# One core, block-sorted attention and a gated MLP: all units in a new order, with other PSUM tiles and copying engines, k loaded before v, and Sinkhorn's matrix kept by rows

## The chip, the core and the metric

The kernel runs on one core of one Trainium2 chip. The core has five engines with their own instruction streams: TensorE (PE in the profile; PEld is its loading of weights), VectorE (DVE), ScalarE (ACT), GpSimd (POOL) and SyncE (SP, which only issues DMAs here). DMAs are issued from SP, ACT and POOL. The metric is device time in microseconds (us) of the whole program, and lower is better. A profiled execution gives a span, the time from the first to the last instruction that the profile shows; the program's own time is a little longer.

## What is computed

The reference, cut to what matters, with 4 batches, 8 heads, 768 tokens, head size 64, 8 blocks of 96 tokens, and a hidden width of 1024:

```python
for _ in range(5):                       # P: one 8 x 8 matrix per batch and head
    P = np.exp(P - np.max(P, axis=-1, keepdims=True))
    P = P / (np.sum(P, axis=-1, keepdims=True) + 1e-09)
    P = P / (np.sum(P, axis=-2, keepdims=True) + 1e-09)
k_sorted = np.einsum('bhij,bhjcd->bhicd', P, k_b)      # blocks mixed by P
v_sorted = np.einsum('bhij,bhjcd->bhicd', P, v_b)
scores = scale * np.matmul(q_b, k_sb.transpose(0, 1, 2, 4, 3))   # inside a block
attn = softmax(scores)
x = np.matmul(attn, v_sb)                # heads side by side: 768 x 512 per batch
h = np.maximum(x @ w_in, 0.0)
u, v = h[..., :512], h[..., 512:]
v_n = (v - mean(v)) / np.sqrt(var(v) + 1e-06)
v_s = np.einsum('ts,bsd->btd', w_spatial, v_n) + b_spatial[None, :, None]
out = (u * v_s) @ w_out
```

## The kernel before, in words

The whole work is cut into some 360 small units, and their order is written out by hand in the string ORDER (lines 18 to 51). A unit is a name and its arguments. The kernel walks through the string and calls the function u_NAME for each (lines 789 to 801), so the string fixes the order of the instructions on every engine at once. Each engine works through its own instructions strictly in that order and waits by semaphores for what it needs.

Most units of PE take one of four PSUM tiles, ps0 to ps3 (line 105, two banks each, one buffer each), fill it with matmuls, and name the engine that copies it out: A is ScalarE, D is VectorE. So `KT:3:D:0:0` is: mix k of batch 0, heads 0 and 1, by P and turn it, in ps3, copied out by VectorE. The next unit on ps3 can't start before that copy has ended. The numbers and letters in the string are thus the choice of tile and engine.

The units that the change and the prediction speak of:

- L loads a tensor by POOL with a cast to bf16 (lines 165 to 188): q, k or v of one batch (768 KB in bf16), the u and v halves of w_in (wu, wv), two halves of w_spatial (wsa, wsb), w_out (wo). LH (349) loads half of q of batch 0 on ACT's queue in fp32, and QC (356) casts it. BI loads the bias; IV (223) sets the columns of ones beside v. Eight semaphores serve POOL's loads in turn, so a load waits on POOL for the landing of the eighth load before it.
- SK (234) is one round of Sinkhorn, on 32 partitions (batch and head) by 64 numbers: an exponential on ACT, and row sum, reciprocal, multiply, column sum, reciprocal, multiply on VectorE. S0 loads sort_net. TB, CO, ID, MA, MB, MC prepare tables, zeros, the identity and masks. DM (227) are matmuls on zeros that keep PE going until the data are there.
- PR (257) spreads P over the partitions, P0 (271) makes the mixing matrices of batch 0 on VectorE, PC (280) copies P out of PSUM, and PD (283) makes those of the other batches on POOL.
- QT and QQ (323, 329) turn q of one or two pairs of heads; QP and QX (362, 373) do this for batch 3 by a copy and a DMA transpose. KT and VT (395, 398) mix and turn k and v; VB (401) turns the mixed v back, for batch 0. For the other batches VM (411) mixes v without turning, and VC (425) moves it to its place (vb) by eight DMAs of 99 KB, on SP's queue.
- SC (439) are the scores of a pair of heads and half of the blocks (eight matmuls, then an exponential by ACT); AT (484) multiplies with v (eight matmuls, then reciprocal and multiply on VectorE, into x).
- XT and XX (516, 541) turn x on PE, XD (507) does it by a DMA transpose on SP.
- VP (552) is the v half of x @ w_in for one or two of six token tiles, UP (594) the u half; ST, LN, LA (570, 579, 585) normalize v; WT and WW (526, 532) turn w_spatial; SP (609) is the product with w_spatial, whose sum with the bias VectorE makes; GT (626) the gating on VectorE (D) or POOL (P); OP, OE, OS (634, 647, 653) the last product, its copy and its store.
- SH, GH, OH, OI, OJ (665 to 702) do the last of batch 3 in finer pieces. CK, CF, LF (713, 728, 734) test that Sinkhorn and softmax stayed in range and load the flag; IF is the branch on it, and general_path (743) is taken if they did not.

In the order before, the head is the Sinkhorn chain beside dummy matmuls; then comes the attention of batch 0 with the mixing of v of batch 1 in between; then the attention of each batch is interleaved with the MLP of the batch before it. The first VP stands in line 27.

## Times and profile before

| | |
|---|---|
| time, median of 3 runs | 155.43 us (155.09 to 156.04) |
| time of the profiled execution | 155.6 us |
| span of the profiled execution | 153.8 us |
| busy share of the span: PE, DVE, ACT, POOL | 95%, 75%, 56%, 26% |
| granted TensorE clock, mean | 0.996 |
| dummy matmuls (DM) | 33, 461 ns each |
| bytes read from HBM, written | 24.78 MB, 6.29 MB |
| DMA engines' busy share, first 18 slices of 40 | 0.9 after the first one |

The profile divides the span into 40 slices of 3.85 us and gives each engine's busy share in tenths. A row of the timeline has a start, a length, an engine, a line of the kernel, an operation with output and inputs, and how many; in brackets stands how long the engine sat idle before it and what ended that. Lines 115, 117, 121 and 123 are the helpers that copy for all units, so their rows are told apart by tile and shape. The chain that ended last is PE for 85% of the span and DMA for 7%, the DMA being the first load of k.

### The profile page before, as it was taken

What the parts mean: (1) busy time and instruction counts of PE and PEld (TensorE: products, weight loads), DVE (VectorE), ACT (ScalarE), POOL (GpSimd) and SP (SyncE); (2) the same over time, 40 slices, a digit from 0 to 9 for tenths busy, and PEclk for the clock granted to TensorE, in tenths of its full rate; (3) what the DMA queues carried; (4) which work ended last, traced back from release to release, by engine and by line L of the source; (5) the groups of instructions that cost most, each with busy time, mean ns of one, the idle gap of its engine ahead of it and who ended that gap; (6) DMA issues with size and microseconds to landing.
All of it is one profiled execution on the core that took longest, in us unless ns stands there. A gap on an engine that the chain in (4) does not pass through costs nothing.

```text
span 153.8 us, 4021 instructions
## 1 busy us (share of the span) xinstructions
PE 146.5 (95%) x1679; PEld 95.6 (62%) x1686; DVE 115.7 (75%) x259; ACT 85.4 (56%) x116; POOL 39.3 (26%) x45
## 2 busy tenths in 40 slices
PE   6997998999999999999999999999999999999991
PEld 2436866764667777456777654656876556774750
DVE  3789889958899976299974886797977639855742
ACT  4345998877879245997777057357650072260040
POOL 7952772292020007000000044000000406103630
PEclk9999999999999999999999999999999999999998
DMA  3999999999999999991069048708608300307746
GB/s 100 251 203 203 204 205 204 210 219 248 220 208 256 203 232 245 208 194 24 0 158 134 19 104 161 190 0 38 191 14 258 121 0 0 136 0 268 288 181 235
DMA packets 30693, 24.36 MB, mean 158 GB/s; under 512 B 10384, under 2 KB 27792, under 8 KB 30672
## 3 DMA queue, kind: packets, MB, share of 16 engines
q0 software_dynamic: 14432, 12.19, 49.1%
q1 hardware_dynamic: 15136, 10.44, 26.4%
q10 hardware_dynamic: 1104, 1.44, 2.8%
q8 instruction: 14, 0.23, 0.6%
q14 instruction: 7, 0.06, 0.1%
HBM read 24.78 MB, written 6.29 MB: 202 GB/s over the span
## 4 chain that ended last, share of the span: by engine, by line
PE 85%; DMA 7%; ACT 2%; DVE 2%; issue 1%; POOL 1%; POOLq 0%; ACTq 0%
PE ps L614 15%; PE ps L559 14%; PE ps L602 14%; PE ps L640 10%; DMA k_in<-in_k_dram 7%; PE ps L493 5%; PE ps L447 5%; PE ps L670 5%; PE ps L388 4%; PE ps L690 3%; PE ps L319 2%; PE ps L415 2%; PE ps L523 2%; ACT ex_all L452 2%; PE ps L536 1%
## 5 line engine op out<-in xcount | busy, mean ns | idle before, releaser
L631 POOL TENSOR_TENSOR gt<-z,u_sb 128x768 bf16<-128x768 f32 x7 | 11.4, 1642 | 76.7 <-DVE z L620 47.4
L452 ACT ACTIVATE ex_all<-ps 96x768 bf16<-96x768 f32 x32 | 24.7, 806 | 5.6 <-PE ps L447 5.3
L614 PE MATMUL ps<-wspT,v_sb 128*128 128x384 bf16 x144 | 25.1, 326 | 0.0
L602 PE MATMUL ps<-xT,w_in_sb 128*128 128x384 bf16 x128 | 22.8, 326 | 0.0
L501 DVE TENSOR_TENSOR x_sb<-ps,rec_all 96x512 bf16<-96x512 f32 x32 | 22.0, 687 | 1.1
L559 PE MATMUL ps<-w_in_sb,xT 128*128 128x512 bf16 x89 | 21.9, 380 | 0.4
L576 DVE BATCH_NORM_STATS2 stats<-v_sb 128x6 f32<-128x512 bf16 x24 | 16.3, 678 | 4.5 <-ACT v_sb L121 4.5
L115 ACT COPY o_sb<-ps 128x1024 f32<-128x1024 f32 (+1 forms) x12 | 10.9, 905 | 14.6 <-PE ps L690 9.1
L614 PEld LDWEIGHTS <-v_sb 128*128 128x128 bf16 x144 | 13.6, 98 | 8.5
L121 ACT ACTIVATE v_sb<-ps 128x1024 bf16<-128x1024 f32 (+1 forms) x11 | 10.3, 947 | 12.2 <-PE ps L559 12.2
L640 PE MATMUL ps<-w_out_sb,gt 128*128 128x256 bf16 x144 | 16.9, 273 | 0.0
L121 ACT ACTIVATE u_sb<-ps 128x768 bf16<-128x768 f32 x12 | 9.7, 811 | 12.7 <-PE ps L602 12.7
L620 DVE TENSOR_TENSOR z<-ps,b_bc 128x768 f32<-128x768 f32 x12 | 11.4, 954 | 6.9 <-PE ps L614 5.1
L602 PEld LDWEIGHTS <-w_in_sb 128*128 128x128 bf16 x128 | 11.8, 97 | 7.2
L640 PEld LDWEIGHTS <-gt 128*128 128x128 bf16 x144 | 13.8, 98 | 2.0
L559 PEld LDWEIGHTS <-xT 128*128 128x128 bf16 x96 | 8.7, 98 | 9.9
L493 PEld LDWEIGHTS <-ex_all 96*128 96x128 bf16 x256 | 10.7, 97 | 4.0 <-issue 0.5
L493 PE MATMUL ps<-vb,ex_all 96*128 96x65 bf16 x256 | 12.6, 193 | 0.5 <-ACT ex_all L452 0.5
L230 PE MATMUL ps<-warm 128*128 128x512 bf16 x33 | 9.7, 461 | 1.3 <-DVE warm L204 1.3
L447 PE MATMUL ps<-qT,kt_all 64*128 64x96 bf16 x256 | 9.7, 204 | 0.7 <-DVE x_sb L501 0.2
L115 ACT CAST kt_all<-ps 128x768 bf16<-128x768 f32 x11 | 8.7, 801 | 2.2 <-PE ps L388 2.2
L447 PEld LDWEIGHTS <-kt_all 64*128 64x128 bf16 x256 | 6.4, 94 | 5.3 <-issue 3.2
...
## 6 DMA issues: line engine op xcount, KB each, us to landing
...
v_in<-in_v_dram POOLq DMA_DIRECT2D x4, 768.0 KB, 21.0
k_in<-in_k_dram POOLq DMA_DIRECT2D x4, 768.0 KB, 23.6
vb<-vm SPq DMA_DIRECT2D x24, 99.0 KB, 5.7
q_in<-in_q_dram POOLq DMA_DIRECT2D x3, 768.0 KB, 28.9
...
w_in_sb<-in_moe_w_in_dram POOLq DMA_DIRECT2D x2, 512.0 KB, 24.7
q<-in_q_dram ACTq DMA_DIRECT2D x1, 768.0 KB, 4.6
```

The lines of the kernel that those rows point to most:

```text
L115: nc.scalar.copy(out=out, in_=in_)
L121: nc.scalar.activation(out=out, in_=in_, func=AF.Relu)
L447: nc.tensor.matmul(t[:, hh, 0:HW].rearrange("p (g x) -> p g x", g=G)[:, :, ii * TB:(ii + 1) * TB], lhsT=kT[rows, i * BLK:i * BLK + 128], r ...
L452: nc.scalar.activation(out=e_tile(b, hp, ih).rearrange("p h (x g) -> p h x g", g=G), in_=t[0:BLK, :, 0:HW].rearrange("p h (g x) -> p h x g ...
L493: nc.tensor.matmul(t[:, hh, ii * VW:ii * VW + D + 1], lhsT=e[:, c:c + 128], rhs=vb[b % 2][:, ih * NI + ii, 2 * hp + hh, 0:D + 1], start=Tr ...
L501: nc.vector.tensor_mul(out=x_sb[:, hp].rearrange("p i (h d) -> p h i d", h=2), in0=tv[:, :, :, 0:D], in1=_raw_ap(rec, 0, [rec.ap[0], [NI, ...
L559: nc.tensor.matmul(t[:, x, :], lhsT=st["xT", b][:, n // 3, kc, (n % 3) * 128:(n % 3 + 1) * 128], rhs=w_in_sb[:, kc, DH:DFF], start=(kc == ...
L576: nc.vector.bn_stats(out=stats, in_=st["v_sb", b, n])
L602: nc.tensor.matmul(t[:, x, 0:HW], lhsT=w_in_sb[:, kc, mc * 128:(mc + 1) * 128], rhs=st["xT", b][:, ih, kc, :], start=(kc == 0), stop=(kc = ...
L614: nc.tensor.matmul(t[:, x, 0:HW], lhsT=st["v_sb", b, n][:, mc * 128:(mc + 1) * 128], rhs=wspT[:, 3 * x:3 * x + 3, n, :], start=(n == 0), s ...
L620: nc.vector.tensor_add(out=z.rearrange("p (x c) -> p x c", x=2), in0=t[:, :, 0:HW], in1=b_bc.rearrange("p (x c) -> p x c", x=2),)
L640: nc.tensor.matmul(t[:, x, c:c + w], lhsT=st["gt", b, mc][:, (n0 + x) * 128:(n0 + x + 1) * 128], rhs=w_out_sb[:, mc, c:c + w], start=(mc = ...
```

## The change

It does three things.

First, a new ORDER. The same work is done: 32 SC and AT, 16 KT and UP, 12 VM and SP, 24 token tiles of VP, 33 dummy matmuls. Some is cut differently: in 15 VP units, not 13; q of batch 1 in four QT, not two QQ; x of batch 1 in two XX, not four XT; w_spatial in two WW and two WT, not three WW. Tiles and copying engines are other ones nearly everywhere. Counted in units, VectorE copies 6 VP, 3 KT, 3 VM, 3 VT and 5 UP (before 2, 5, 5, 1 and 4), ScalarE 9, 13, 9, 1 and 11 (before 11, 11, 7, 3 and 12). PC moves from VectorE to ScalarE. IV:1 moves to the end, OE of one tile to VectorE, the last four DMAs of batch 3's VC and three of the stores to ACT's queue, and all stores behind the loading of the flag. The part after the first SH is as before.

Second, loads. Before: v, k, rest of q (batch 0), then v, q, k (batch 1), wv, wsb, wu, v of batch 2, wsa, q of batch 2, the bias, k of batch 2. After: k, v, rest of q, then v, k, q, wv, wu, v, k, q of batch 2, wsa, wsb, the bias. The last ones (q of batch 3, wo, v and k of batch 3) stay in that order. The identity (ID) now stands ahead of the first load on POOL, and the first PD ahead of k of batch 1.

Third, Sinkhorn keeps its matrix by rows, in place: the tile p_cols goes, the first multiply writes p_all as it lies, the column sum reads it in steps, and the last multiply reads it as it lies.

```diff
 ORDER = """
-S0 L:v:0:0:8 LH:A:0 TB CO SK:0 BH ID IV:2 SK:1 SK:2 MA L:k:0:0:8 L:q:0:4:8 DM:3:6:512 DM:0:6:512 L:v:1:0:8 L:q:1:0:8
-QC:A:0 SK:3 QC:A:1 MB SK:4 DM:2:6:512 DM:1:6:512 MC QT:2:D:0:1 DM:1:6:512 DM:3:3:512 PR:1 L:k:1:0:8 QT:2:A:0:0 P0:0:2
-L:wv L:wsb P0:4:6 P0:6:8 IV:0 P0:2:4 PC:D VT:0:A:0:0 KT:3:D:0:0 L:wu PD:1:0:4 VT:2:A:0:1 L:v:2:0:8 KT:1:A:0:3
-KT:0:D:0:2 SC:2:0:0:1 VB:3:D:0:0 PD:1:4:8 KT:1:A:0:1 QT:0:D:0:2 IV:1 QT:2:A:0:3 VB:3:D:0:1 SC:0:0:1:0 VT:1:D:0:3
-VT:2:A:0:2 L:wsa L:q:2:0:8 SC:3:0:0:0 PD:3:0:4 PD:3:4:8 BI AT:0:0:0:1 L:k:2:0:8 VB:1:D:0:3 SC:2:0:1:1 AT:3:0:0:0
-VM:0:A:1:0 VB:1:D:0:2 SC:2:0:2:0 AT:3:0:1:0 SC:0:0:3:0 AT:1:0:2:0 SC:2:0:2:1 AT:3:0:1:1 VM:0:A:1:2 AT:2:0:3:0
-XT:1:A:0:0:0 VM:0:D:1:3 QQ:3:D:1:2 SC:1:0:3:1 VM:2:D:1:1 XT:0:A:0:1:0 KT:1:A:1:2 L:q:3:0:8 AT:3:0:3:1 VC:1:4:8
-KT:0:A:1:1 AT:2:0:2:1 KT:1:A:1:0 VC:1:0:4 QQ:3:D:1:0 KT:0:A:1:3 PD:2:0:4 XT:2:D:0:0:2 XT:1:D:0:1:2 PD:2:4:8 L:wo
-SC:3:1:0:1 SC:0:1:2:0 VP:2:D:0:0:1 ST:0:0 SC:0:1:1:1 SC:1:1:3:1 ST:0:1 VP:3:A:0:4:5 VP:2:A:0:2 VP:1:A:0:3 ST:0:5
...
+S0 LH:A:0 TB CO SK:0 BH ID SK:1 L:k:0:0:8 IV:0 MA SK:2 DM:0:6:512 DM:0:6:512 SK:3 QC:A:0 SK:4 DM:0:6:512 DM:0:6:512
+QT:0:D:0:0 DM:1:6:512 MC QC:A:1 DM:1:3:512 PR:1 MB P0:2:4 P0:6:8 P0:0:2 P0:4:6 PC:A QT:2:A:0:1 L:v:0:0:8 KT:3:A:0:1
+KT:0:D:0:3 KT:2:A:0:0 VT:1:D:0:0 L:q:0:4:8 KT:3:A:0:2 VT:0:D:0:1 L:v:1:0:8 SC:2:0:0:1 VB:1:D:0:0 SC:3:0:0:0 SC:0:0:1:1
+PD:1:0:4 L:k:1:0:8 QT:2:D:0:3 QT:1:D:0:2 VT:3:A:0:3 AT:2:0:0:1 SC:0:0:3:0 VB:1:D:0:1 SC:3:0:2:0 AT:2:0:0:0 PD:1:4:8
+SC:0:0:1:0 VT:1:D:0:2 VM:3:A:1:1 VB:2:D:0:3 VM:0:A:1:0 AT:1:0:1:1 SC:3:0:3:1 VB:2:D:0:2 VM:0:A:1:3 AT:1:0:3:0
+SC:3:0:2:1 VM:2:D:1:2 KT:0:A:1:2 AT:1:0:1:0 KT:3:A:1:0 KT:2:A:1:1 AT:0:0:2:0 KT:1:A:1:3 L:q:1:0:8 L:wv AT:3:0:2:1
+XT:2:A:0:1:0 XT:0:D:0:0:0 IV:2 XT:1:A:0:0:2 AT:3:0:3:1 L:wu L:v:2:0:8 QT:2:A:1:0 QT:0:D:1:3 L:k:2:0:8 QT:1:A:1:1
+VC:1:4:8 QT:3:D:1:2 XT:2:D:0:1:2 L:q:2:0:8 SC:0:1:0:1 SC:1:1:0:0 SC:3:1:1:1 VC:1:0:4 VP:2:D:0:2:3 ST:0:3 PD:2:4:8
...
+LA:1:1 OE:A:0:0 LA:1:5 UP:2:A:2:1:0 VM:1:D:3:0 XD:2:1 LA:1:3 ST:2:1 VC:3:0:4:0:4 VP:3:A:2:0:4 LA:1:4 VP:0:A:2:3:5
+ST:2:4 SC:2:3:3:0 ST:2:0 SC:1:3:2:0 ST:2:5 SP:3:1:1 ST:2:3 SC:0:3:1:0 SC:2:3:1:1 SP:1:1:0 ST:2:2 AT:3:3:2:0 OP:0:0:2:2
...
-    p_cols = const.tile([BH, NB, NB], FP32, name="p_cols")
...
-        nc.vector.tensor_mul(out=p_cols.rearrange("p j i -> p i j"), in0=p_all, in1=over_rows(rowsum))
-        nc.vector.reduce_sum(out=cols, in_=p_cols, axis=AX.X)
+        nc.vector.tensor_mul(out=p_all, in0=p_all, in1=over_rows(rowsum))
+        nc.vector.reduce_sum(out=cols, in_=p_all.rearrange("p i j -> p j i"), axis=AX.X)
...
-        nc.vector.tensor_mul(out=to, in0=p_cols.rearrange("p j i -> p i j"), in1=over_cols(colsum))
+        nc.vector.tensor_mul(out=to, in0=p_all, in1=over_cols(colsum))
```

46 lines of the change are left out of this document (23 added, 23 removed).

## The prediction

> **What bounds the kernel now.** I read the page first, then the busy time by stretches, then TensorE's own rows in order of time, and then the issues of the loads on POOL.
>
> ```profile
> PE 146.5 (95%) x1679; PEld 95.6 (62%) x1686; DVE 115.7 (75%) x259; ACT 85.4 (56%) x116; POOL 39.3 (26%) x45
> PE   6997998999999999999999999999999999999991
> DVE  3789889958899976299974886797977639855742
> ACT  4345998877879245997777057357650072260040
> ```
>
> TensorE is busy 95% of the 153.8 us, and before the last slice its row has gaps only in the first seven, of 3.85 us each. There ACT and DVE stand at 8 and 9 as well. The stretches say it in numbers:
>
> ```profile
> 12.90:32.70 19.80, 18.31 (x433) 14.67 (x433) 18.01 (x34) 17.58 (x24) 10.47 (x12) 1.00 1.28 205
> 32.70:60.00 27.30, 27.22 (x346) 17.93 (x347) 22.30 (x45) 17.40 (x24) 6.28 (x7) 1.00 1.25 229
> 60.00:100.00 40.00, 39.59 (x458) 25.77 (x459) 30.12 (x55) 27.05 (x36) 3.88 (x3) 1.00 0.68 124
> 100.00:137.40 37.40, 37.24 (x308) 24.76 (x310) 28.70 (x70) 16.10 (x21) 4.89 (x3) 1.00 0.31 78
> ```
>
> The columns are length, PE, PEld, DVE, ACT and POOL busy, then granted clock, DMA share and GB/s. From 12.9 to 32.7 PE is busy 18.31 of 19.80 us, with DVE at 18.01 and ACT at 17.58: three engines that hand four PSUM tiles to one another, each about 90% full. From 32.7 on PE leaves only 0.08, 0.41 and 0.16 us free in 104.7 us, at a granted clock of 1.00. So a new order can win in the first stretch, and in the rest it can almost only lose.
>
> ```profile
> 12.01 0.35 PE L260 MATMUL ps<-p_t,spread 32*128 32x32 bf16 x8 [0.39 <-DVE p_t L255]
> 12.87 0.53 PE L388 MATMUL ps<-pd,v_in 128*64 128x128 bf16 x12
> 13.68 0.53 PE L388 MATMUL ps<-pd,k_in 128*64 128x128 bf16 x12 [0.28 <-DMA k_in<-in_k_dram]
> 32.68 1.89 PE L559 MATMUL ps<-w_in_sb,xT 128*128 128x512 bf16 x7
> 137.37 7.96 PE L670 MATMUL ps<-wspT,v_sb 128*128 128x512 bf16 x48
> ```
>
> These rows cut the span into four: the head up to 12.87, where the Sinkhorn chain sets the pace (PE waits for p_t); stage 1 up to the first VP at 32.68; stage 2 up to the first SH at 137.37, 104.69 us; and the tail of 16.43 us. A transfer holds PE up only once, for 0.28 us, at the first k.
>
> **The change, part by part.** *Sinkhorn in place.* Per round the same operations remain; the multiply now writes contiguously, and the column sum reads in steps.
>
> ```profile
> 11.80 0.51 DVE L117 COPY qT<-ps 128x768 bf16<-128x768 bf16 x1
> L247 DVE TENSOR_TENSOR p_cols<-p_all,rowsum 32x64 f32<-32x64 f32 x5 | 1.3, 261 | 0.2
> L253 DVE TENSOR_TENSOR p_all<-p_cols,colsum 32x64 f32<-32x64 f32 x4 | 1.0, 255 | 0.1
> L248 DVE TENSOR_REDUCE colsum<-p_cols 32x8 f32<-32x64 f32 x4 | 0.8, 207 | 0.1
> L218 DVE CAST mask<-m 128x16 bf16<-128x16 f32 x1 | 0.2, 152 | 0.0
> ```
>
> Before, L247 wrote in steps (261 ns) and L253 read in steps (255 ns), so steps cost at most the 6 ns between them. I take 0. The bounds are -0.03 us (five rounds of 6 ns saved) and +0.27 us (the reduction rising to a multiply's 261 ns, 54 ns in each of five rounds). MB, 0.15 us, moves from a gap of the chain to behind the copy of q, ahead of P0; that copy ends at 12.31 as now, and P0 starts behind both, some 0.02 us later than now. The casts QC fit between the exponentials as before. The first unit of stage 1 (now a KT) starts at 12.87 to 12.90.
>
> *Loads: k first, then v.* What the loads do now:
>
> ```profile
> 1.25 1.06 POOL L171 DMA_DIRECT2D v_in<-in_v_dram  x1 [0.80 <-POOLq L816]
> 2.31 0.22 POOL masks.py:197 MEMSET ident<- 128x128 bf16 x1
> 2.61 0.29 POOL masks.py:199 TENSOR_SCALAR_AFFINE_SELECT ident<-ident 128x128 bf16<-128x128 bf16 x1
> 7.21 0.80 POOL L176 DMA_DIRECT2D w_in_sb<-in_moe_w_in_dram  x1
> 10.11 0.80 POOL L179 DMA_DIRECT2D w_in_sb<-in_moe_w_in_dram  x1 [1.14 <-DMA v_in<-in_v_dram]
> 23.88 0.62 POOL L200 DMA_DIRECT2D b_bc<-in_moe_b_spatial_dram  x1 [0.49 <-DMA q_in<-in_q_dram]
> 27.73 0.89 POOL L171 DMA_DIRECT2D k_in<-in_k_dram  x1 [3.23 <-DMA k_in<-in_k_dram]
> 36.94 0.88 POOL L171 DMA_DIRECT2D v_in<-in_v_dram  x1 [2.37 <-DMA w_in_sb<-in_moe_w_in_dram]
> DMA to landing us min/median/max: 22.8/24.7/26.5
> 2.96 10.67 DMA k_in<-in_k_dram
> 29.25 27.77 SPq L428 DMA_DIRECT2D vb<-vm  x16
> vb<-vm SPq DMA_DIRECT2D x24, 99.0 KB, 5.7
> k_in<-in_k_dram POOLq DMA_DIRECT2D x4, 768.0 KB, 23.6
> ```
>
> POOL waits for the eighth load before a new one, so these waits date landings: v0 10.1, q1 23.9, k1 27.7, wu 36.9; the chain gives k0 as 13.6, and the landing line of w_in gives wv as 7.21 + 22.8 = 30.0. The stream is full: one load of 768 KB takes 27.73 - 23.88 = 3.85 us, whenever it was issued. So a load's landing follows from its place. In the new order the identity (0.54 us from 2.31 to the end of its pair's issue) goes ahead of the first load, so places shift by 0 (the stream is full anyway) to 0.54 us: k0 10.1 to 10.6, v0 13.6 to 14.2, v1 about 20, k1 takes q1's place at 23.9 to 24.4, q1 takes k1's at 27.7 to 28.3, wv keeps 30.0 to 30.5. k1 is now issued behind the first PD, which waits for PC; PC on ACT ends about 12.8, the PD (1.1 us) 13.9, and k1 is issued by 14.9, five microseconds before its turn: 0. wsb no longer goes ahead of wu; wu lands earlier than now. Later loads come in the same sum of bytes from BI on: 0.
>
> *Stage 1.* Both orders do the same units before the first VP; the new one does one score unit SC more (three of batch 1, not two). What it re-deals is who frees which PSUM tile.
>
> ```profile
> 12.92 0.80 ACT L115 COPY qT<-ps 128x768 bf16<-128x768 bf16 x1 [2.33 <-PE ps L319]
> 80.37 2.21 ACT L452 ACTIVATE ex_all<-ps 96x768 bf16<-96x768 f32 x3
> L115 ACT CAST kt_all<-ps 128x768 bf16<-128x768 f32 x11 | 8.7, 801 | 2.2 <-PE ps L388 2.2
> L117 DVE CAST kt_all<-ps 128x768 bf16<-128x768 f32 x5 | 4.8, 954 | 1.0 <-PE ps L388 0.8
> 39.28 0.28 PE ps L447 x8
> ```
>
> ACT with work ready starts one of 0.81 us every 0.70 (three in 2.21). I followed each unit through its PSUM tile: a unit starts when the copy that last held its tile has ended, a copy when PE and its engine's previous work are done. In the new order ACT has 24 copies and exponentials from the copy of q at 12.93 (now 12.92) to that of QT:1:A:1:1, the last one before VP that holds a tile. I take 0.71: 23 steps are 16.33; the tiles make ACT wait 0.48 more (SC:3:0:0:0 and VT:3:A:0:3 cost 0.13 each, the rest less). It starts that copy at 29.74 and ends it at 30.54; two SC of 0.28 follow, and VP:2 stands at **31.3** (its tile, freed by DVE's XT copy at 31.1, is no later). Now it is at 32.68 with as many instructions on ACT (24): the old order leaves ACT waiting 2 us more. Nothing in the rows guarantees the ideal; I give back 0.5 us for small waits, and for v0, v1, k1 and q1, needed at 14.2, 20.5, 24.2 and 28.5 and landing within 0.3 us of it: VP at **31.8**, -0.88, between 30.8 (no waits) and 32.7 (as now).
>
> *Transfers beside it.* VC:1 (eight of 99 KB) is issued when the last VM of batch 1 is copied: by the same following at 25.6, not 29.25. Its bytes take 792/768 of 3.85, 3.97 us of the stream, from whatever load is under way. Now VC:1 starts 0.75 us before wv lands, and wu, due behind wsb (by bytes 30.0 + 2.9 + 2.6 = 35.5), comes 1.4 late, 7.7 us after the first VC. In the new order wv is due 4.4 to 4.9 us after it, so by that slope (1.4 in 7.7) 0.8 to 0.9 late: 30.8 to 31.4, needed at 31.3. I take 0 beyond the 0.5; the bound is all 3.97 us on wv. The Trainium skill's page DMA: Bandwidth & Descriptors, section Queues, rings and completion order, says that each DMA engine takes turns between queue rows packet by packet. It speaks against this change: VC's row would take half the stream from 25.6 on, and wv would land near 34, not 31; the trace, with wu 1.4 us late and not nearly 4, bears it out only in part.
>
> *Stage 2.* The total of PE's units is unchanged; one SC (0.28) is already done: -0.28.
>
> ```profile
> L121 ACT ACTIVATE v_sb<-ps 128x1024 bf16<-128x1024 f32 x9 | 9.2, 1026 | 11.9 <-PE ps L559 11.9
> L123 DVE TENSOR_SCALAR v_sb<-ps 128x1024 bf16<-128x1024 f32 x2 | 2.4, 1224 | 2.8 <-PE ps L559 2.8
> 91.37 2.51 SPq L428 DMA_DIRECT2D vb<-vm  x4
> DMA to landing us min/median/max: 2.8/5.7/7.1
> ```
>
> Copies go from ACT to DVE (VP pairs: four on DVE at 1.22, not two; two single ones and two XX besides; KT and VM two fewer each, VT two more): summed by these prices ACT loses about 4 us of its 85 and DVE gains about 3 of 116, so DVE stays under 80%: nothing on the path as a whole. The cover is thinnest in batch 3: VC:3:0:4 waits for VM:1:D:3:0, copied by a DVE that runs 2.5 us behind PE there, about 54.8 us after the first VP; four issues (2.51) and a landing (2.8) end at 60.1, and AT:3:3:2:0 is due at 60.8. 0.7 us of cover; if it is gone PE waits the difference. XX, WT and QP find tiles 0.2 to 0.4 us ahead of PE. I take +0.4 for stage 2 (0 to 1.5): 104.69 - 0.28 + 0.4 = 104.81. Nothing changes from SH to the end; the extra early stores (two of 512 KB that now wait for the flag) find the DMA share at 0.31 over 100 to 137: 0.
>
> **Sum.** 31.8 + 104.81 + 16.43 = 153.04 us of span, against 153.8. The profiled execution took 155.6, so 1.8 lies around its span: 154.84. It stood 0.17 above the median of 155.43: **154.7 us**.
>
> **The rivals.** *More:* none of the 0.9 us that I gave back is lost: 31.3 + 104.41 + 16.43 + 1.63 = 153.8, and 153.3 without ACT's 0.48. For it speaks that each tile's release was placed; against it, 1.5 us of PE waits in the same stretch now that a planner surely did not want.
>
> *Nothing:* the change doesn't do what it says, since what it guards against hardly happens: PE waits for a transfer 0.28 us in all. The full stretch then stays at 19.8 us, its waits only move: 32.68 + 104.81 + 16.43 + 1.63 = 155.55; about 155.4.
>
> *Slower, by VC:1 in front of wv:* place, the first VP, which reads w_in's v half. Price, all 3.97 us of VC:1's bytes on wv: 30.0 + 0.5 + 3.97 = 34.4; then 34.4 + 104.81 + 16.43 + 1.63 = 157.3. It decides from a landing of wv after 31.8, and the kernel is slower than before from about 32.6. For it: VC:1 starts 3.7 us earlier, and PE itself comes 1 us sooner. Against it: wu's delay now is 1.4 of 4. The Trainium skill's page DMA: Bandwidth & Descriptors, in the same section, points to this rival: taking turns gives wv at 34.0 without the 0.5 (an estimate).
>
> **How the numbers follow.** The forecast (154.0 to 155.1) 0.40, more (below 153.9) 0.19, nothing (155.1 to 156.3) 0.25, slower by wv 0.16, most of it above 157.0. The range goes from the sum without waits, 153.3, to the slower rival's 157.3; the forecast alone would be 154.0 to 155.1. Differences under 1% (153.9 to 157.0) are about what a measurement here can't tell from no change: faster 0.19, same 0.68, slower 0.13.
>
> **What would show it.** Right: the first L559 row near 31.8 with no DMA in front of it; 12.9 to 31.8 with ACT above 90%; first L388 reading k_in at 12.9 without a DMA wait; 104.8 us from that L559 to the first L670. Wrong: a PE wait on w_in_sb, k_in, q_in or v_in between 14 and 36; a wait at L493 on vb near 92; p_t later than 11.86; DVE ahead of PE's waits after 60 us.

## The result, and the profile after

The changed kernel takes 157.71 us (median of five runs, 156.39 to 157.95), beside 155.6 us for the kernel before on the same chip (155.09 to 156.05): ratio 1.0117, 95% interval 1.0076 to 1.0158. It is slower by 1.2%, where 154.7 us and no measurable difference were forecast. Its profiled execution took 156.39 us, the fastest of its runs, with a span of 154.6 us; 1.8 us lie around the span, as in the kernel before. TensorE's granted clock was 0.996 to 1.00 in all profiles but two of the experiments (GT on VectorE; warm-up in several tiles), where its mean was 0.69 to 0.86 in stretches between 12.8 and 20 us, so that their stage 1 is some 1.3 us too long and isn't used. Over the whole span these two profiles show 0.987 and 0.989, and some of the timed runs show as little (0.985 to 0.989): one of these five, and three of the six of each kernel in which only the warm-up was edited (a5_fewer_dummies, a10_dm_tiles).

The page of the changed kernel, as its busy shares and its 40 slices, and then the stretches cut at its own first KT, first VP and first SH (length, PE, PEld, DVE, ACT, POOL, clock, DMA share, GB/s):

```profile
PE 145.9 (94%) x1686; PEld 95.1 (62%) x1686; DVE 120.7 (78%) x264; ACT 81.5 (53%) x113; POOL 41.1 (27%) x46
PE   6986999999999999996999999999999999999991
```

```profile
12.76:32.90 20.14, 18.43 (x441) 14.95 (x441) 17.56 (x34) 18.17 (x26) 15.23 (x18) 1.00 1.29 209
32.90:60.00 27.10, 27.03 (x372) 17.76 (x373) 21.59 (x42) 20.72 (x28) 2.82 (x4) 1.00 1.24 230
60.00:100.00 40.00, 38.75 (x423) 25.22 (x423) 34.93 (x69) 21.83 (x29) 8.30 (x5) 1.00 0.64 110
100.00:138.17 38.17, 37.84 (x313) 25.09 (x311) 30.15 (x63) 13.71 (x18) 5.14 (x4) 1.00 0.27 88
```

TensorE's slices have a new 6 at the nineteenth, and the stretch from 60 to 100 us, which left 0.41 us free before, now leaves 1.25. TensorE's rows in order of time say where:

```profile
12.76 0.86 PE L388 MATMUL ps<-pd,k_in 128*64 128x128 bf16 x24 [0.16 <-DVE pd L274]
14.92 0.53 PE L388 MATMUL ps<-pd,k_in 128*64 128x128 bf16 x12 [1.30 <-ACT qT L116]
31.92 0.33 PE L523 MATMUL ps<-ident,x_sb 96*128 96x96 bf16 x4 [0.30 <-issue]
32.90 3.61 PE L559 MATMUL ps<-w_in_sb,xT 128*128 128x512 bf16 x16
72.00 2.12 PE L614 MATMUL ps<-wspT,v_sb 128*128 128x384 bf16 x12 [1.25 <-DVE x_sb L501]
138.17 7.96 PE L670 MATMUL ps<-wspT,v_sb 128*128 128x512 bf16 x48
```

There are two long waits, 1.30 us in front of the third KT and 1.25 us in front of an SP. Neither is a transfer. The first KT starts at 12.76 without a wait for k (before: 0.28 us of it), the first VP at 32.90 and not at 31.8, the first SH 105.27 us later and not 104.81, and the tail has its 16.43 us.

**The first wait.** ScalarE, VectorE and POOL just ahead of it:

```profile
12.28 1.42 DVE L274 TENSOR_TENSOR pd<-mask,ps 128x256 bf16<-128x256 bf16 x4
13.79 0.37 ACT L116 CAST prep_sb<-ps 128x256 bf16<-128x256 f32 x1 [2.64 <-DVE pd L274]
14.06 0.80 ACT L116 COPY qT<-ps 128x768 bf16<-128x768 bf16 x1
14.25 1.09 POOL L286 TENSOR_TENSOR pd<-mask,prep_sb 128x512 bf16<-128x512 bf16 x1 [9.08 <-ACT prep_sb L116]
```

PC, the cast of P out of ps1, is on ScalarE now. In the kernel before it was one more VectorE instruction behind VectorE's four P0, which read the same tile:

```profile
13.73 0.41 DVE L117 CAST prep_sb<-ps 128x256 bf16<-128x256 f32 x1
```

On ScalarE it starts only when the last P0 is done, at 13.70, here and in all other profiles with PC on ScalarE: the program puts these two readers of one PSUM tile in order. ScalarE sat idle for 2.64 us, and behind PC in its queue stood the copy of q's second pair. That copy holds ps2, which the third KT wants, and it starts at 14.06 and not at the 12.93 of the prediction.

**The second wait.** VectorE and POOL around 70 us, and all copies into the tile qp:

```profile
69.02 2.09 DVE L118 COPY qp<-q_in 128x768 bf16<-128x768 bf16 x2
69.26 3.35 POOL L631 TENSOR_TENSOR gt<-z,u_sb 128x768 bf16<-128x768 f32 x2 [20.05 <-DVE z L620]
71.03 0.19 DVE L500 RECIPROCAL rec_all<-ps 96x8 f32<-96x8 f32 x1
71.26 0.69 DVE L501 TENSOR_TENSOR x_sb<-ps,rec_all 96x512 bf16<-96x512 f32 x1
```

```profile
L118 DVE COPY qp<-q_in x3: 327/350/1821, 69.0 to 74.5; 128x768 bf16<-128x768 bf16 x3
```

The columns of the last line are shortest, median and longest in ns. One copy of three took 1821 ns where its like take 327 and 350. It started at 69.29, just behind the first of POOL's two gate multiplies (3.35 us for two; the first 1.63, until 70.89), and ended just behind it, at 71.11. The reciprocal and multiply that free ps0 stood behind it, and the SP on ps0 waited. This too is a choice of engine that the change made: in the kernel before, the QP of pairs 1, 2 and 3 are on ScalarE.

### The profile page after: what moved, and what is told of

Read it like the earlier page. It is cut to its first block, busy times and chain, and to the rows that moved or that the text cites. A ratio compares the mean times of both kernels' runs of the same rounds, so it can differ in the third digit from the quotient of the medians.

```text
span 154.6 us, 4039 instructions
## 1 busy us (share of the span) xinstructions
PE 145.9 (94%) x1686; PEld 95.1 (62%) x1686; DVE 120.7 (78%) x264; ACT 81.5 (53%) x113; POOL 41.1 (27%) x46
## 4 chain that ended last, share of the span: by engine, by line
PE 77%; DVE 14%; ACT 4%; issue 2%; ACTq 0%; DVEq 0%
PE ps L614 13%; PE ps L602 12%; PE ps L559 11%; PE ps L640 10%; PE ps L493 6%; PE ps L670 5%; PE ps L388 4%; PE ps L447 4%; PE ps L690 3%; PE ps L319 2%; DVE gt L631 2%; PE ps L415 2%; ACT vm L116 1%; PE ps L406 1%; DVE qp L118 1%
## 5 line engine op out<-in xcount | busy, mean ns | idle before, releaser
L452 ACT ACTIVATE ex_all<-ps 96x768 bf16<-96x768 f32 x32 | 24.2, 803 | 14.0 <-PE ps L447 13.8
L631 POOL TENSOR_TENSOR gt<-z,u_sb 128x768 bf16<-128x768 f32 x8 | 13.3, 1669 | 59.4 <-DVE z L620 47.4
L602 PE MATMUL ps<-xT,w_in_sb 128*128 128x384 bf16 x128 | 23.1, 326 | 0.1
L559 PE MATMUL ps<-w_in_sb,xT 128*128 128x512 bf16 x96 | 22.7, 379 | 0.1
L116 ACT COPY o_sb<-ps 128x1024 f32<-128x1024 f32 (+1 forms) x11 | 9.6, 894 | 20.5 <-PE ps L640 11.3
L640 PE MATMUL ps<-w_out_sb,gt 128*128 128x256 bf16 x144 | 16.7, 273 | 0.0
L602 PEld LDWEIGHTS <-w_in_sb 128*128 128x128 bf16 x128 | 11.9, 97 | 7.2
L122 ACT ACTIVATE u_sb<-ps 128x768 bf16<-128x768 f32 x11 | 8.9, 811 | 11.1 <-PE ps L602 11.1
L493 PE MATMUL ps<-vb,ex_all 96*128 96x65 bf16 x256 | 11.9, 193 | 0.1
L683 POOL TENSOR_TENSOR gt<-z,u_sb 128x512 bf16<-128x512 f32 (+1 forms) x5 | 5.2, 1056 | 21.3 <-DVE z L676 21.2
L588 DVE TENSOR_SCALAR v_sb<-v_sb,mv,rstd 128x512 bf16<-128x512 bf16 x24 | 10.1, 459 | 0.6 <-ACT rstd L583 0.6
L116 ACT CAST kt_all<-ps 128x768 bf16<-128x768 f32 x13 | 9.9, 803 | 0.3 <-PE ps L388 0.3
L122 ACT ACTIVATE v_sb<-ps 128x1024 bf16<-128x1024 f32 (+1 forms) x9 | 7.5, 835 | 4.5 <-PE ps L559 4.4
```

The source lines that it names most:

```text
L116: nc.scalar.copy(out=out, in_=in_)
L122: nc.scalar.activation(out=out, in_=in_, func=AF.Relu)
L452: nc.scalar.activation(out=e_tile(b, hp, ih).rearrange("p h (x g) -> p h x g", g=G), in_=t[0:BLK, :, 0:HW].rearrange("p h (g x) -> p h x g ...
L493: nc.tensor.matmul(t[:, hh, ii * VW:ii * VW + D + 1], lhsT=e[:, c:c + 128], rhs=vb[b % 2][:, ih * NI + ii, 2 * hp + hh, 0:D + 1], start=Tr ...
L559: nc.tensor.matmul(t[:, x, :], lhsT=st["xT", b][:, n // 3, kc, (n % 3) * 128:(n % 3 + 1) * 128], rhs=w_in_sb[:, kc, DH:DFF], start=(kc == ...
L602: nc.tensor.matmul(t[:, x, 0:HW], lhsT=w_in_sb[:, kc, mc * 128:(mc + 1) * 128], rhs=st["xT", b][:, ih, kc, :], start=(kc == 0), stop=(kc = ...
```

## The experiments

Times are medians; "ratio" is that of a kernel's runs to the runs of the kernel before on the same chip, with its interval. Four profiles of the changed kernel, two of the kernel before and one of each experiment give this table (one profile is one execution, and some fell on the fastest of their kernel's runs); its columns are the start of the first stage 1 unit, the lengths from there to the first VP, to the first SH and to the end, and the span, all in us.

| kernel | first unit | to VP | to SH | to end | span |
|---|---|---|---|---|---|
| before | 12.87 / 12.87 | 19.81 / 20.02 | 104.69 / 104.69 | 16.43 / 16.42 | 153.8 / 154.0 |
| changed, 1st | 12.76 | 20.14 | 105.27 | 16.43 | 154.6 |
| changed, 2nd (a0_again) | 13.42 | 20.30 | 105.54 | 16.44 | 155.7 |
| changed, 3rd (a0_third) | 13.70 | 20.04 | 105.27 | 16.39 | 155.4 |
| changed, 4th (a0_fourth) | 12.99 | 20.08 | 105.59 | 16.44 | 155.1 |
| PC on VectorE (a1_pc_dve) | 13.09 | 19.46 | 105.54 | 16.41 | 154.5 |
| two QP on ScalarE (a2_qp_act) | 13.12 | 20.04 | 104.95 | 16.39 | 154.5 |
| both (a3_both) | 12.77 | 19.44 | 104.67 | 16.42 | 153.3 |
| PC behind q on ScalarE (a4_pc_behind_q) | 12.75 | 19.88 | 105.89 | 16.38 | 154.9 |
| three warm-up matmuls fewer (a5_fewer_dummies) | 12.77 | 20.05 | 105.16 | 16.92 | 154.9 |
| warm-up in several tiles (a10_dm_tiles) | 12.75 | (21.37) | 105.84 | 17.14 | 157.1 |
| GT on VectorE (a6_gt_dve) | 12.84 | (21.47) | 105.15 | 16.44 | 155.9 |
| PC, two QP, warm-up, VT (a8_all) | 12.76 | 19.45 | 104.57 | 16.72 | 153.5 |
| PC, three QP, tiles (a11_four) | 12.76 | 19.99 | 104.70 | 17.15 | 154.6 |
| the same, loads early (a12_loads_early) | 12.75 | 20.00 | 104.28 | 16.67 | 153.7 |
| head mended alone (a14_head) | 12.75 | 20.70 | 105.18 | 17.07 | 155.7 |
| everything mended (a13_best) | 12.75 | 19.72 | 104.74 | 17.09 | 154.3 |
| VC behind the first VP (a9_vc_behind_vp) | 13.37 | 20.46 | 105.88 | 16.39 | 156.1 |
| before, with Sinkhorn by rows (b1_sk_rows) | 12.83 | 20.06 | 104.69 | 16.42 | 154.0 |

### The two waits

The changed kernel once more, as the base:

> The changed kernel once more. Its profiled run was its fastest, span 154.6 us; its other runs had spans of 155.7 to 156.2. A profile of a typical run should show where that 1.3 us lies. Theory of transfers: a wait of TensorE for a load (w_in's v half or k of batch 1) in stage 1 that the first profile did not have. Theory of waits between engines alone: the same rows as in the first profile, and the time at the first VP and at the first SH within 0.2 us of 32.9 and 138.2. Time 157.7 by both.

157.75 us, ratio 1.0102 (1.0066 to 1.0137). The two waits stand as before (1.30 and 1.25 us), and there is no wait for a transfer. The theory of transfers falls. But the prediction of the same rows at the same times falls too: everything from P's product on is 0.66 us later. That is taken up below.

PC on VectorE, as in the kernel before:

```diff
-P0:4:6 PC:A QT:2:A:0:1
+P0:4:6 PC:D QT:2:A:0:1
```

> The changed kernel, with the cast of P's product (PC) on VectorE behind its four P0, as in the kernel before, and not on ScalarE. Theory of the shared tile: ScalarE then copies q's second pair at about 12.9 and not at 14.06, the KT in tile 2 starts near 13.8 and not at 14.92, and the first VP comes 0.7 to 1.1 us earlier (VectorE has 0.4 us more to do ahead of KT:0). About 156.8. Rival, transfers: w_in's v half landed at about 32.2 in the first profile, so that VP can come no earlier than that: -0.7 at most, with a DMA wait in front of it. Rival, cover: the stretch is bound by the copies of both engines, VectorE's 0.4 us more take the gain back, and the first VP stays at 32.7 to 32.9: 157.5.

156.62 us, ratio 1.0028 (0.9989 to 1.0067), 1.13 us less than the changed kernel on the same chip. Its copy of q on ScalarE, and TensorE's next units:

```profile
13.07 0.80 ACT L116 COPY qT<-ps 128x768 bf16<-128x768 bf16 x1 [1.93 <-PE ps L319]
```

```profile
13.09 1.36 PE L388 MATMUL ps<-pd,k_in 128*64 128x128 bf16 x36
14.66 0.53 PE L388 MATMUL ps<-pd,v_in 128*64 128x128 bf16 x12 [0.22 <-DMA v_in<-in_v_dram]
```

The copy now waits for its own matmuls only, three KT run without a gap (x36), and the 1.30 us are gone. What comes next in line is a transfer: 0.22 us for v of batch 0. Stage 1 takes 19.46 us, 0.6 to 0.8 less than in the four profiles of the changed kernel.

Two of the copies QP on ScalarE, also as in the kernel before:

```diff
-QP:D:3:1 VC:2:4:8:0:4 QP:D:3:3
+QP:A:3:1 VC:2:4:8:0:4 QP:A:3:3
```

> The changed kernel, with two of the copies QP (batch 3, pairs 1 and 3) on ScalarE and not on VectorE, so that none stands beside POOL's multiply at 69.3. Theory of the blocked copy: TensorE's wait of 1.25 us ahead of the SP in tile 0 near 72 goes; 156.5. Rival: ScalarE, which now has two copies of 0.83 us more in front of the exponentials, gives a wait of its own of the same size at the next AT: 157.7. Rival: the time given back is met by the next wait in line (a transfer, or VectorE's statistics), -0.3 to -0.6.

156.49 us, ratio 1.0035 (0.9997 to 1.0073), 1.26 less than the changed kernel on the same chip. In the profile the 1.25 us at the SP are gone and a wait of 0.43 us for VectorE's x stands at the next L602 row, so that 0.3 to 0.6 us of stage 2 are saved. What else differs from a0_again's profile lies in the head and in stage 1, ahead of the edit, so that the share of the 1.26 us that this edit made isn't shown exactly. Of the expectations, the first and the third are both partly right.

Does the copy suffer from POOL, or has VectorE simply too much to do? The next run gives VectorE more work, and takes one gate multiply from POOL:

```diff
-GT:P:0:2 SC:3:2:0:1
+GT:D:0:2 SC:3:2:0:1
```

> The changed kernel, with the first gate multiply of batch 0 that POOL runs (GT:P:0:2) on VectorE, at its place; the two copies QP stay on VectorE. VectorE so has 0.96 us more to do, not less. Theory of the blocked copy: with no POOL multiply beside it the second copy takes 0.35 and not 1.82 us, and TensorE's wait of 1.25 us at the SP in tile 0 goes: 156.5, and 0.3 later where VectorE runs behind. Rival, load: VectorE simply has too much to do here; then the copy stays long or the wait moves, and the time is 157.7 or more.

156.78 us, ratio 1.0082 (1.005 to 1.0114). The interval reaches into that of the changed kernel, so the time alone doesn't decide; the rows of POOL and then VectorE do:

```profile
68.78 1.64 POOL L631 TENSOR_TENSOR gt<-z,u_sb 128x768 bf16<-128x768 f32 x1 [18.15 <-ACT ex_all L452]
```

```profile
71.05 0.62 DVE L118 COPY qp<-q_in 128x768 bf16<-128x768 bf16 x2
71.58 0.20 DVE L500 RECIPROCAL rec_all<-ps 96x8 f32<-96x8 f32 x1
73.40 0.96 DVE L631 TENSOR_TENSOR gt<-z,u_sb 128x768 bf16<-128x768 f32 x1
```

POOL's multiply has ended at 70.42, before the copies start. The two take 0.62 us together, not 2.09, and TensorE's wait of 1.25 us is gone although VectorE does 0.96 us more. So it is POOL's instruction beside the copy, not VectorE's load. Stage 2 takes 105.15 us all the same: 0.43 us for VectorE's x stand at the next L602 row, and 0.55 us that nothing named ends at an L529 row. The Trainium skill's page SBUF — State Buffer, section Who interferes with whom, says that copies of VectorE in certain fast modes and GpSimd share a pair of ports, and that whoever comes second is blocked for the whole instruction of the other. The trace agrees: 1821 ns for the copy that started 0.03 us behind a POOL multiply of 1.63 us, 350 for the one that started 0.24 us ahead of it, and 327 with none beside it.

Both edits in one kernel:

> Both edits, PC on VectorE and the two QP on ScalarE. If the two waits are the cause and independent, the gains add: 157.7 - 0.9 - 1.25 = 155.5, as the kernel before or a little below it. If both only uncover a transfer or the copies' sum, the gain is that of the larger one alone or less: 156.5 to 157.5.

156.17 us, ratio 0.9994 (0.9959 to 1.0029): level with the kernel before, 1.58 us less than the changed kernel. The gains add only in part, and the profile has the transfers where the two waits were. TensorE, then POOL:

```profile
14.57 0.53 PE L388 MATMUL ps<-pd,v_in 128*64 128x128 bf16 x12 [0.55 <-DMA v_in<-in_v_dram]
24.94 0.53 PE L388 MATMUL ps<-pd,k_in 128*64 128x128 bf16 x12 [0.15 <-DMA k_in<-in_k_dram]
```

```profile
32.27 0.93 POOL L171 DMA_DIRECT2D q_in<-in_q_dram  x1 [1.13 <-DMA w_in_sb<-in_moe_w_in_dram]
```

v of batch 0 is waited for until 14.57, k of batch 1 until 24.94, and w_in's v half lands by 32.27, just as the first VP (32.21) wants it. Stage 2 takes 104.67 us, where 104.81 were predicted.

PC left on ScalarE, but behind the copy of q:

```diff
-P0:4:6 PC:A QT:2:A:0:1
+P0:4:6 QT:2:A:0:1 PC:A
```

> The changed kernel, with PC still on ScalarE, but behind the copy of q's second pair instead of in front of it. Theory of the shared tile and the queue: what cost 1.1 us was that the copy of q stood behind a cast that waited for VectorE; the copy of q then starts some 0.3 us after its transposes begin to land (about 12.7 to 13.1), PC at about 13.8, and the time is that of PC on VectorE, 156.6 (156.3 to 156.9). Rival, engine: ScalarE lacks the 0.37 us of the cast itself; then only VectorE helps, and this stays at 157.4 to 157.7.

157.15 us, ratio 1.0104 (1.0069 to 1.014): in time no gain that can be told, against the first expectation. ScalarE did what was expected:

```profile
12.64 0.80 ACT L116 COPY qT<-ps 128x768 bf16<-128x768 bf16 x1 [1.50 <-PE ps L319]
13.73 0.37 ACT L116 CAST prep_sb<-ps 128x256 bf16<-128x256 f32 x1 [0.29 <-DVE pd L274]
```

The wait of 1.30 us is gone here too. But TensorE then waits 0.58 us for v of batch 0 and 0.45 us for v of batch 1 (at 21.55), and stage 1 takes 19.88 us. So the queue in front of the copy of q made the wait; that mending it there is worth 1.1 us isn't shown, since transfers take most of it back in this profile.

### Sinkhorn by rows, alone in the kernel before

```diff
-        nc.vector.tensor_mul(out=p_cols.rearrange("p j i -> p i j"), in0=p_all, in1=over_rows(rowsum))
-        nc.vector.reduce_sum(out=cols, in_=p_cols, axis=AX.X)
+        nc.vector.tensor_mul(out=p_all, in0=p_all, in1=over_rows(rowsum))
+        nc.vector.reduce_sum(out=cols, in_=p_all.rearrange("p i j -> p j i"), axis=AX.X)
```

> The kernel before with only the change of the Sinkhorn loop: P written by rows, the column sum read in steps. Per round the two multiplies fall from 261 and 255 to 211 ns and the reduction rises from 207 to 254, so p_t is ready about 0.2 us earlier (11.65, not 11.86). Reading one: TensorE waits for p_t before P's product, so the first VT starts 0.2 earlier; but the first KT waits for k of batch 0 at 13.68 anyway, and the gain ends there: 0 to -0.1 us. Reading two: the gain goes through, -0.2. Reading three: the stretch is bound by the warm-up matmuls (ending at 11.63 in the profile), -0.15 at most. 155.3 to 155.6 by all of them, so what is to be read is the trace.

155.66 us, ratio 0.9998 (0.9962 to 1.0034). P is ready at 11.64 and not at 11.86, as in the changed kernel. TensorE's rows:

```profile
9.91 2.12 PE L229 MATMUL ps<-warm 128*128 128x512 bf16 x9
11.95 0.36 PE L259 MATMUL ps<-p_t,spread 32*128 32x32 bf16 x8
```

P's product no longer waits for P but for the warm-up matmuls, the first 24 of which took 8.23 us here, and the first VT starts at 12.83, only 0.04 us earlier. So the gain ends at the warm-up, as in reading three; behind it the first KT waits for k until 13.80, so a gain that got past the warm-up would have ended there, as in reading one.

### The late head

The 33 warm-up matmuls (DM) run ahead of P's product in both orders. A third profile of the changed kernel and a second of the kernel before:

> A third profile of the changed kernel. Its median is 1.3 us above its fastest run. If the lateness of the typical run lies in the head (TensorE's warm-up matmuls ending late), the first KT is late by what the span is above 154.6, up to 13.4, and the rest is as in the first two profiles: 20.1 to 20.3 us to the first VP, 105.2 to 105.6 to the first SH. If it lies in instruction supply along the way, there are idle stretches of TensorE of 0.2 to 0.6 us that no engine and no transfer ends, at places that differ from profile to profile.

> A second profile of the kernel before. Its head has slack: TensorE waits 0.18 us for q_in and 0.39 us for p_t. So late warm-up matmuls should show as a shorter wait for p_t, with P's product still at 12.0 and the first VP at 32.7, span 153.8. By the other reading (the new order is not more exposed than the old one) its first KT or VT moves by as much as in the changed kernel.

157.23 us with a span of 155.4, and 155.89 us with a span of 154.0. TensorE's first rows in the changed kernel, then in the kernel before:

```profile
1.28 8.57 PE L230 MATMUL ps<-warm 128*128 128x512 bf16 x24 [1.28 <-DVE warm L204]
10.00 0.53 PE L319 MATMUL ps<-ident,q_in 128*64 128x128 bf16 x12
10.46 2.33 PE L230 MATMUL ps<-warm 128*128 128x512 bf16 x9
12.85 0.35 PE L260 MATMUL ps<-p_t,spread 32*128 32x32 bf16 x8
```

```profile
1.29 6.73 PE L230 MATMUL ps<-warm 128*128 128x512 bf16 x24 [1.29 <-DVE warm L204]
9.05 0.53 PE L319 MATMUL ps<-ident,q_in 128*64 128x128 bf16 x12 [1.03 <-ACT q_in L115]
9.51 2.12 PE L230 MATMUL ps<-warm 128*128 128x512 bf16 x9
12.01 0.35 PE L260 MATMUL ps<-p_t,spread 32*128 32x32 bf16 x8 [0.39 <-DVE p_t L255]
```

The first 24 took 8.57 us here and 6.73 there; in the four profiles of the changed kernel it was 7.28 to 8.57, and in the three of the old order (with b1_sk_rows) 6.73 to 8.23. So the old order has late ones too; it has room for them. The next nine take 2.33 us in the changed order in every profile, 2.12 in the old one. The old order waits for P (0.39 us); in the changed one P, ready at about 11.7, waits for TensorE until 12.85. A possible reason can be read in the two orders: in the changed one the groups of warm-up matmuls stand in tiles 0, 0, 0, 0, then 1 and 1, and the transposes and P's product take the same tiles; the old order has them in 3, 0, 2, 1, then 1 and 3. If a group waits for the end of the group before it in its tile, the changed order pays for that. Two experiments:

```diff
-DM:0:6:512 DM:0:6:512 ... DM:0:6:512 DM:0:6:512 QT:0:D:0:0 DM:1:6:512 MC QC:A:1 DM:1:3:512 PR:1
+DM:3:6:512 DM:2:6:512 ... DM:1:6:512 DM:3:6:512 QT:0:D:0:0 DM:1:6:512 MC QC:A:1 DM:2:3:512 PR:1
```

> The changed kernel with its 33 warm-up matmuls in PSUM tiles 3, 2, 1, 3, then 1 and 2, and not in 0, 0, 0, 0, then 1 and 1. Theory: a group of them waits until the last matmul of the group before it in the same tile has ended; that costs about 0.2 us at the first copy's transposes, 0.2 between the last two groups and 0.1 at P's product, and up to 0.2 at each of the first groups, so the head of the typical run is 0.5 us earlier: the last nine take 2.12 and not 2.33, the first KT stands at 12.8 to 13.0, the median at 157.2. Rival: the lateness is that of TensorE's instruction supply alone (the first 24 took from 7.28 to 8.57 us in the same kernel); then the tiles change nothing and the median stays at 157.7.

```diff
-QC:A:1 DM:1:3:512 PR:1
+QC:A:1 PR:1
```

> The changed kernel without DM:1:3:512, the last three of the 33 warm-up matmuls, 0.64 us of TensorE directly ahead of P's product. In four profiles of the changed order the 24 first of them ended at 8.56, 8.69, 9.23 and 9.56 us, and P's product, ready to start at 11.65, started at 11.80, 11.81, 12.23 and 12.56. Theory: the new order has no slack for late warm-up matmuls, so its typical run starts stage 1 up to 0.66 us late; without the three, 0.3 to 0.6 off the median: 157.2, and the first KT at 12.8 (12.7 to 13.0). Rival: the head's delay is covered by the next wait (v of batch 0, landing near 14.5): 157.6. Rival: TensorE's clock falls without them: slower.

In the tiles' run the nine take 2.12 us again, and P's product waits for P:

```profile
9.38 2.12 PE L230 MATMUL ps<-warm 128*128 128x512 bf16 x9
11.80 0.35 PE L260 MATMUL ps<-p_t,spread 32*128 32x32 bf16 x8 [0.30 <-DVE p_t L255]
```

So the tiles cost 0.21 us there, as expected. In the other run the first 24 took 8.50 us and the first KT still stood at 12.77. But the times don't follow: 157.9 us, ratio 1.011 (1.005 to 1.017), and 157.34 us, ratio 1.0126 (1.0088 to 1.0164); the three runs of each at a clock of 1.00 have medians of 157.01 and 156.97. Both were timed on other chips than the changed kernel, so two runs on one chip were added, the changed kernel and one with both edits:

> The changed kernel as the base for the next two runs on the same chip: 157.7, its first KT between 12.8 and 13.7.

> The changed kernel with its warm-up matmuls in several tiles and the last three left out, PC and QP as they are. If the head's delay goes through to the end, 0.5 us less than the changed kernel on this chip (0.3 to 0.7), first KT at 12.76. If it is taken up on the way (by v of batch 0 and of batch 1, and w_in's v half, which land when they land), the same time within 0.15.

157.42 us, ratio 1.0122 (1.0067 to 1.0178), and 157.39 us, ratio 1.0104 (1.0057 to 1.015). The second expectation holds: with the first KT at 12.75 the time is the same. In the profile of the mended one TensorE stands idle elsewhere, with nothing named that ends it:

```profile
20.83 0.38 PE L406 MATMUL ps<-ident,vt_all 128*128 128x128 bf16 x4 [0.67 <-issue]
```

That the head is late in the changed order is shown; that it costs time is not.

### Transfers

```diff
-VC:1:4:8 QT:3:D:1:2 ... VC:1:0:4 VP:2:D:0:2:3
+QT:3:D:1:2 ... VP:2:D:0:2:3 VC:1:4:8 VC:1:0:4
```

> The changed kernel, with the sixteen copies of batch 1's values (VC:1) issued behind the first VP instead of from 26.7 us on; one profile, for the landing of w_in's v half, which ended POOL's wait at 32.1 to 32.3 in three profiles. Theory of taking turns: VC's queue took half the stream in front of w_in, and without it the half lands near 30.2, two us earlier. Theory of the prediction: VC delays it by 0.8 to 0.9, so it lands near 31.3. If it stays at 32.2, the stream was simply later than worked out and VC costs it nothing. The time gains nothing here, since the first VP stands behind 32.7 anyway; VC later may cost a wait at the AT of batch 1 from 36 on.

157.94 us, span 156.1. The edit did not do what it was meant for: SP's queue has nothing else to wait for there, and it issued the copies at 27.30 as soon as the values were there (26.68 in the changed kernel, whose first KT is 0.61 earlier). The run is one more profile of the changed kernel and says nothing on what VC:1 costs.

Three kernels go on from the one with both waits mended. The first leaves out three warm-up matmuls (as above) and moves a VT:

```diff
-VT:1:D:0:0 L:q:0:4:8 KT:3:A:0:2 VT:0:D:0:1
+L:q:0:4:8 KT:3:A:0:2 VT:1:D:0:0 VT:0:D:0:1
```

> All that has helped, and one step more: PC on VectorE, two QP on ScalarE, three warm-up matmuls fewer, and VT of pair 0 behind the fourth KT, since with both waits gone TensorE waited 0.55 us there for v of batch 0 (landing near 14.5). If those are the waits that end last: PC and QP together gave 156.2, the head gives 0.3 to 0.6 and the VT 0.3 to 0.5 more: 155.3 (154.9 to 155.7), at or below the kernel before. If the transfers as a whole bound stage 1 (k of batch 1, w_in's v half near 32.2), the first VP stays at 32.2 and the time at 156.

The second has the warm-up in several tiles (as above) and a third QP on ScalarE:

```diff
-QP:D:3:2 SP:0:0:3
+QP:A:3:2 SP:0:0:3
```

> PC on VectorE, three QP on ScalarE (batch 3, pairs 1, 2 and 3), and the warm-up matmuls in several tiles. With PC and two QP the median was level with the kernel before (ratio 0.999). If the gains add: 0.2 to 0.4 for the head, and the wait of 0.43 us at the L602 row near 75.5 goes: 155.5, ratio 0.995 to 0.997. If transfers now end last in stage 1 (v of batch 0 at 14.5, w_in at 32.2), only the 0.4 behind them comes through: ratio 0.997 to 0.999.

The third is the second with the loads of batch 1 and w_in's v half issued early:

```diff
-PD:1:0:4 L:k:1:0:8 QT:2:D:0:3 ... KT:1:A:1:3 L:q:1:0:8 L:wv AT:3:0:2:1
+L:k:1:0:8 L:q:1:0:8 L:wv PD:1:0:4 QT:2:D:0:3 ... KT:1:A:1:3 AT:3:0:2:1
```

> The kernel of the run before this one, with k and q of batch 1 and w_in's v half issued ahead of the first PD (from about 6 us on, as POOL is free) and not at 15.2, 17.2 and 18.1. The prediction's reading, a full stream that lands loads in the order of issue: k of batch 1 at 24.9 and w_in's half at 32.2 as now, the time within 0.1 of the run before. Rival, loads in flight share the stream: the early ones land earlier (w_in's half near 30), v of batch 0 later than 14.5, and the time moves by the difference at the first VT: +0.5 to +2. Second rival: the stream had gaps while POOL was late with issues; then all land earlier, the first VP comes up to 0.5 us sooner.

a8_all: 156.11 us, ratio 1.0029 (0.9999 to 1.0059). Moving VT only exchanged its wait for others (0.18 us for a KT's tile, 0.45 us for VectorE's copy of v). a11_four: 156.18 us, ratio 1.0012 (0.9978 to 1.0046); the wait at L602 fell from 0.43 to 0.28, and v of batch 0 was waited for 1.03 us, until 15.04. a12_loads_early: 156.23 us, ratio 1.0015 (0.9981 to 1.005). Its first issue of w_in, and POOL's wait for that load:

```profile
6.87 0.80 POOL L176 DMA_DIRECT2D w_in_sb<-in_moe_w_in_dram  x1
```

```profile
32.79 0.93 POOL L171 DMA_DIRECT2D q_in<-in_q_dram  x1 [1.05 <-DMA w_in_sb<-in_moe_w_in_dram]
```

Issued at 6.87 us instead of 18.06, w_in's half landed at 32.8, and not at 31.9 as in a11_four; v of batch 0 landed at 15.07 and k of batch 1 at 25.56. These loads land in the order of issue, and not earlier when they are issued earlier; both rivals fall.

Everything at once:

```diff
-QC:A:1 DM:1:3:512 PR:1 MB ... PC:A ... VT:1:D:0:0 L:q:0:4:8 KT:3:A:0:2 VT:0:D:0:1 ... QP:D:3:1 ... QP:D:3:3 ... QP:D:3:2
+QC:A:1 PR:1 MB ... PC:D ... L:q:0:4:8 KT:3:A:0:2 VT:1:D:0:0 VT:0:D:0:1 ... QP:A:3:1 ... QP:A:3:3 ... QP:A:3:2
```

with the warm-up in tiles 3, 2, 1, 3 and 1.

> Everything mended: the head as in the run before, PC on VectorE, three QP on ScalarE, and the first VT behind the fourth KT. Sum from the traces of its parts: first KT 12.76, first VP 32.2 (w_in's half lands there), 104.5 to the first SH, 16.4 to the end: span 153.1, 154.9 to 155.3 in time; the kernel before stands at 155.4 to 155.7. If transfers land late on this chip (v of batch 0 at 15.0), 155.6 to 156.2, level.

155.59 us, ratio 0.9994 (0.9957 to 1.0031). Level, as for late transfers. The first KT is where it was expected; k of batch 1 is waited for until 25.37, the first VP stands at 32.47 (32.2 expected), stage 2 takes 104.74 (104.5), and 0.50 us stand idle in the tail in front of L690. No version beat the kernel before by what can be measured.

## Why the prediction was wrong

It said 154.7 us, a gain, and 157.71 were measured, a loss. Two waits that it did not have make the changed kernel slower than the one before: without them (a3_both) it is level. They do not explain all that was missed, since a3_both still stands at 156.17, 1.5 us above the forecast. That its profile has a span of 153.3 us, near the 153.04 of the sum, is luck: it fell on the fastest of twelve executions (155.20). So the forecast gain isn't there with both waits mended either. Step by step:

- *Sinkhorn in place, 0, between -0.03 and +0.27 us.* Wrong by 0.2, outside of its bounds. Before, each of the two multiplies had one stepped operand, so the 6 ns between them told nothing of a multiply with none: that takes 211 ns, not 255 to 261, and the reduction that now reads in steps 254, not 207.

```profile
L247 DVE TENSOR_TENSOR p_all<-p_all,rowsum 32x64 f32<-32x64 f32 x5 | 1.1, 211 | 0.2
L248 DVE TENSOR_REDUCE colsum<-p_all 32x8 f32<-32x64 f32 x4 | 1.0, 254 | 0.1
L253 DVE TENSOR_TENSOR p_all<-p_all,colsum 32x64 f32<-32x64 f32 x4 | 0.8, 212 | 0.1
```

  Two multiplies by -45 and a reduction by +47 make some -45 ns in a round, and P is ready 0.21 us earlier. In the old order no gain in time came of it (b1_sk_rows), and in the changed one P's product waits for the warm-up.
- *"The first unit of stage 1 starts at 12.87 to 12.90."* 12.76 in the fastest profile, 12.99 to 13.70 in the other three. The prediction counted the same 33 warm-up matmuls and did not look at their tiles, nor at how much later than in the profile of before the first 24 can end.
- *"PC on ACT ends about 12.8, the PD 13.9, and k1 is issued by 14.9."* This is the step that failed first. PC ended at 14.16, PD at about 15.3, and k of batch 1 was issued at 15.29. The prediction had VectorE's P0 and ScalarE's PC side by side on one tile. Each unit was followed through the tile that it takes, but PC takes none; it reads one that another engine is reading. Its copy of q's second pair, due at 12.93, so started at 14.06, and TensorE waited 1.30 us. Putting PC back on VectorE takes 1.13 us off the median (a1_pc_dve), of which 0.6 to 0.8 show in stage 1 of the profiles.
- *The first VP at 31.8.* 32.90 in the first profile; 32.21 with both waits mended. (Its working has a slip of 0.2 us: 30.54 and two SC of 0.28 are 31.1, not 31.3, which makes the miss larger.) In that last profile TensorE waits 0.70 us for transfers in this stretch; no run takes them away, so that they make the remaining 0.4 us is argued, not shown. The prediction named them ("v0, v1, k1 and q1, needed at 14.2, 20.5, 24.2 and 28.5 and landing within 0.3 us of it"), but had them too early: v of batch 0 came at 14.57 to 15.07 (said: 13.6 to 14.2), k of batch 1 at 24.94 to 25.56 (said: 23.9 to 24.4), w_in's half at 31.9 to 32.8 in the profiles whose first KT is at 12.76 (said: 30.8 to 31.4). Its rule "a load's landing follows from its place" held (a12_loads_early); the start of the stream didn't. GB/s by slice, the kernel before and then the changed one:

```profile
GB/s 100 251 203 203 204 205 204 210 219 248 220 208 256 203 232 245 208 194 24 0 158 134 19 104 161 190 0 38 191 14 258 121 0 0 136 0 268 288 181 235
```

```profile
GB/s 103 221 189 203 204 207 202 208 246 230 204 205 211 258 258 227 201 202 44 181 156 70 0 105 6 92 13 4 0 79 124 4 0 173 331 222 396 113 174 235
```

  In the second and third slice (3.85 to 11.6 us) the changed order moves 30 and 14 GB/s less, 0.17 MB, which is 0.8 us at 204 GB/s; the other profiles of that order have 218 to 241 and 180 to 202 there. 0.2 us of it is the first load's later issue (1.45, not 1.25); what takes the rest stays open. It isn't the number of loads under way: with k, q and w_in's half issued by 7.7 us the two slices have 236 and 184 (a12_loads_early).
- *Stage 2, "XX, WT and QP find tiles 0.2 to 0.4 us ahead of PE", +0.4.* Wrong by 0.5 to 0.8 us: 105.27 to 105.59 and not 104.81. The tiles were found; what stood behind the QP on VectorE, the multiply that frees ps0, was not asked for, and the 1.25 us at the SP came of it. "DVE ahead of PE's waits after 60 us" was one of the prediction's own signs of being wrong. The prediction summed durations from rows without a neighbour on POOL. The profile of before had a warning, a gate multiply of VectorE of 2.01 us at 90.38 beside one of POOL, where its like take 0.95:

```profile
89.93 1.64 POOL L631 TENSOR_TENSOR gt<-z,u_sb 128x768 bf16<-128x768 f32 x1 [29.33 <-ACT u_sb L121]
```

```profile
90.38 2.01 DVE L631 TENSOR_TENSOR gt<-z,u_sb 128x768 bf16<-128x768 f32 x1
```

- *"0.7 us of cover" for VC:3:0:4.* Right: no wait on vb near 94. *The tail, 16.43:* right.
- *The rival "slower, by VC:1 in front of wv".* The sign was right and the mechanism wrong: no profile has a wait of TensorE for w_in. The half was 1.4 to 2.8 us later than its place without VC:1 (30.0 to 30.5), of which the slow start of the stream is likely a part. Where the section Queues, rings and completion order of the Trainium skill's page DMA: Bandwidth & Descriptors would have put it, near 34 by the prediction's estimate, it never landed. What VC:1 costs was not measured (a9_vc_behind_vp).

What stays open: PC and QP together give 1.58 of the 2.0 us by which the medians differ (157.75 and 155.75 on that chip). The rest isn't settled, and neither is the 1.5 us between the mended kernel and the forecast. The late head and idle stretches without a named end are seen in the profiles, and mending the head alone gave nothing.
